# Computing M behind the denominators of a linear-attention kernel, in halves and single PSUM banks

## The chip, the core and the metric

One core of a Trainium2 chip runs the whole kernel. The metric is the device time of one execution in microseconds (us). Times are medians of three to six runs; the runs of the kernel before lay between 211.77 and 212.39 us beside the changed kernel. With one core there is no second die to compare, and every run used here was classed as fast.

Engines as the profile names them: PE is the matmul engine (TensorE), PEld its weight loads, DVE is VectorE, ACT is ScalarE, SP issues the DMAs. PSUM, where matmuls write, has eight banks.

## The reference, cut to what matters

```python
xn  = layernorm(x)                                  # 2048 tokens, D = 640
pq, pk = phi(q), phi(k)                             # phi(t) = 1e-6 + (t+1 where t>0, else exp(t)); 32 heads of 20
kv  = einsum("bhsd,bhse->bhde", pk, v)
num = einsum("bhqd,bhde->bhqe", pq, kv)
den = einsum("bhqd,bhd->bhq", pq, sum_s(pk)) + 1e-6
return x + (num / den) @ wo + gelu(xn @ w1 + b1) @ w2 + b2
```

The kernel never forms `num`. It multiplies the small block-diagonal `kv` by `wo` once, giving a 640x640 matrix **M**, and scales the rows of `pq` by 1/den. Each tile of 128 output tokens is then one accumulation in a pair of PSUM banks: 12 pairs of matmuls with W2 (the dense part), then 5 pairs of PQ·M.

## The kernel before: the parts that matter

```python
def q_chunk(c):                       # 512 tokens of q: 5 units, each 5 matmuls of 128x512
    for j in range(DT):
        b = take(1)                   # next bank of the ring of eight
        ...                           # matmuls into bank b
        phi(bank(b), b, 1, PQ[:, j, cc], r_PQ[c][j], [])   # ACT exp, then two DVE operations; frees b

def m_step():
    for j in range(DT):
        b = take(2)                   # a pair of banks
        for h in range(2):
            for i in range(2):
                for q in range(4):    # four matmuls on 32 columns of the array each
                    c0 = j + 32 * DT * q
                    fns.append(... e.matmul(bank(b + h, 0, HW)[32*q:32*q+32, :],
                        KVT[:, q + i, c0:c0 + 31*DT + 1:DT], Wo[:, q + i, h*HW:(h+1)*HW], ...))
        Pl.ins("tensor", fns, reads=[r_KVT, r_Wo], writes=B_[b:b + 2])
        Pl.ins("scalar", ... e.activation(halves(Msb[:, j, :]), pair(b), ACT.Copy),   # the eviction
               reads=B_[b:b + 2], writes=[r_M[j], r_zsum, r_zhl])
...                                   # cut
q_chunk(0); z_step(); kvt_step(); q_chunk(1); q_chunk(2)
m_step()
q_chunk(3)
...                                   # cut: inputs loaded again for the residual
bs = [out_w2(0)]                      # tile 0, W2 part
db = den_step()                       # 20 matmuls on 32 columns; DVE adds 1e-6, then the reciprocal
bs += [out_w2(1), out_w2(2, 0, JT // 2)]
rden_step(0, db)                      # broadcasts 1/den by a matmul; ACT copies, DVE scales PQ
out_w2(2, JT // 2, JT, bs[2])
for t in range(3):
    out_fin(t, bs[t])                 # PQ·M, residual, store
...                                   # cut: tiles 3 to 15, one after the other
```

A planner puts in the semaphore waits from the lists `reads` and `writes`. Each engine except PE also waits for its own earlier instruction where both write the same resource. Every eviction of M lists `r_zsum` and `r_zhl`, because M is stored over those buffers; so every eviction waits for the one before it (**self-wait**).

Of the kernel before, what the change touches and what calls it, by code (L numbers as in the profile page):

```python
# [6 lines left out]
ACT = mybir.ActivationFunctionType  # L7
# [105 lines left out]
def bass_parallel_sum__linear_attn_block__dense_activation_gelu__prompt_kernel(  # L113
# [4 lines left out]
    NT = S // P  # L118
# [3 lines left out]
    DT = D // P  # L122
    JT = F // P
    H = 32
    DH = D // H
    HW = D // 2
# [3 lines left out]
    Pl = Planner(nc)  # L130
# [6 lines left out]
    with contextlib.ExitStack() as es:  # L137
# [14 lines left out]
        KVT = W1f[:, DT * D:2 * DT * D].rearrange("p (k d) -> p k d", k=DT)  # L152
        Wqkv = sb("Wqkv", [P, DT, 3 * D], BF16)
        W2 = sb("W2", [P, JT, D], BF16)
        Wo = sb("Wo", [P, DT, D], BF16)
        Mf = sb("Msb", [P, DT * D], BF16)
        Msb = Mf[:].rearrange("p (k d) -> p k d", k=DT)
# [24 lines left out]
        B_ = [R_("bank%d" % i) for i in range(8)]  # L182
        ring = [0]

        def take(n):
            b = ring[0]
            if n == 2 and b % 2:
                b += 1
            b %= 8
            ring[0] = (b + n) % 8  # L190
            return b

        def bank(b, lo=0, hi=512):
            return ps[:, b * 512 + lo: b * 512 + hi]

        def pair(b):
            return ps[:, b * 512:(b + 2) * 512].rearrange("p (a n) -> p a n", a=2)[:, :, 0:HW]

        def halves(ap):
            return ap.rearrange("p (a n) -> p a n", a=2)  # L200
# [8 lines left out]
        r_Wq, r_Wk, r_Wv, r_W2, r_Wo = R_("Wq"), R_("Wk"), R_("Wv"), R_("W2"), R_("Wo")  # L209
# [11 lines left out]
        r_KVT = R_("KVT")  # L221
        r_M = [R_("M%d" % j) for j in range(DT)]
        r_zsum, r_zhl, r_z, r_ZB = R_("zsum"), R_("zhl"), R_("z"), R_("ZB")
# [30 lines left out]
        for c in range(2, NC):  # L254
# [18 lines left out]
               reads=[r_ident], writes=[r_ident])  # L273
# [108 lines left out]
        def h_first(jbs):  # L382
# [7 lines left out]
            for jb, b in zip(jbs, bs):  # L390
# [6 lines left out]
               reads=[r_warm], writes=[r_b1c])  # L397
# [47 lines left out]
        for t in range(TD, NT):  # L445
            if t > TD:
                ln_next(t)
            Pl.ins("sync", lambda e, t=t: e.dma_start_transpose(xnT[:, :, t * P:(t + 1) * P], xn_tm[:, t, :]),
                   reads=[r_xn[t]], writes=[r_xnT[t]], dma=True)
# [22 lines left out]
        for t in range(NT):  # L472
            b = take(2)
            fns = []
# [10 lines left out]
        for f in range(DT):  # L485
            b = take(2)
            for t in range(NT):
# [3 lines left out]
                    reads=[r_xn[t], r_PK[t]], writes=B_[b:b + 2])  # L491
            Pl.ins("scalar", lambda e, b=b, f=f: e.activation(halves(GTb[:, f, :]), pair(b), ACT.Copy),
                   reads=B_[b:b + 2], writes=[r_GT[f]] + r_W1)

        Pl.ins(v, lambda e: e.tensor_tensor(out=zsum, in0=PK[:, 0, :], in1=PK[:, 1, :], op=ALU.add),
               reads=[r_PK[0], r_PK[1]], writes=[r_zsum])
        for t in range(2, NT):
            Pl.ins(v, lambda e, t=t: e.tensor_tensor(out=zsum, in0=zsum, in1=PK[:, t, :], op=ALU.add),  # L498
                   reads=[r_PK[t], r_zsum], writes=[r_zsum])
# [3 lines left out]
               reads=[r_zsum, r_zhl], writes=[r_zhl])  # L503


        def q_chunk(c):
            cc = slice(c * CW, (c + 1) * CW)
            for j in range(DT):
                b = take(1)
                Pl.ins("tensor", [(lambda e, k=k, j=j, b=b: e.matmul(  # L510
                    bank(b), Wqkv[:, k, j:D:DT], xnT[:, k, cc],
                    start=(k == 0), stop=(k == DT - 1))) for k in range(DT)],
                    reads=[r_Wq] + r_xnT[c * CH:(c + 1) * CH], writes=[B_[b]])
                phi(bank(b), b, 1, PQ[:, j, cc], r_PQ[c][j], [])
# [20 lines left out]
                    out=KVT[:, t, e0[t]:e1[t]], in0=bank(b, 0, Wd[t]), in1=maskKV[t][:], op=ALU.mult),  # L535
                    reads=[B_[b], r_masks], writes=[r_KVT])

        def m_step():
            for j in range(DT):
                b = take(2)  # L540
                fns = []
                for h in range(2):
                    for i in range(2):
                        for q in range(4):
                            c0 = j + 32 * DT * q
                            fns.append(lambda e, t=q + i, q=q, i=i, h=h, b=b, c0=c0: e.matmul(  # L546
                                bank(b + h, 0, HW)[32 * q:32 * q + 32, :],
                                KVT[:, t, c0:c0 + 31 * DT + 1:DT], Wo[:, t, h * HW:(h + 1) * HW],
                                start=(i == 0), stop=(i == 1)))
                Pl.ins("tensor", fns, reads=[r_KVT, r_Wo], writes=B_[b:b + 2])  # L550
                Pl.ins("scalar", lambda e, b=b, j=j: e.activation(halves(Msb[:, j, :]), pair(b), ACT.Copy),
                       reads=B_[b:b + 2], writes=[r_M[j], r_zsum, r_zhl])

        def den_step():
            b = take(1)
            Pl.ins("tensor", [(lambda e, j=j, c=c: e.matmul(  # L556
                bank(b)[H * c:H * (c + 1), :], ZB[:, j, :], PQ[:, j, c * CW:(c + 1) * CW],
                start=(j == 0), stop=(j == DT - 1))) for j in range(DT) for c in range(NC)],
                reads=[r_ZB] + [r for q in r_PQ for r in q], writes=[B_[b]])
            Pl.ins(v, lambda e: e.tensor_single_scalar(den_sb[:], bank(b), 1e-6, ALU.add),  # L560
                   reads=[B_[b]], writes=[r_den])
            Pl.ins(v, lambda e: e.reciprocal(rden[:], den_sb[:]), reads=[r_den], writes=[r_rden])

            return b

        def rden_step(c, b):
            cc = slice(c * CW, (c + 1) * CW)
            s = c % 3
            rs = ek[:, s, 0:CW]
            Pl.ins("tensor", lambda e: e.matmul(bank(b), E4[:, c, :], rden[:], start=True, stop=True),  # L570
                   reads=[r_E4, r_rden], writes=[B_[b]])
            Pl.ins("scalar", lambda e: e.activation(rs, bank(b), ACT.Copy), reads=[B_[b]], writes=[r_ek[s]])  # L572
            for j in range(DT):
                Pl.ins(v, lambda e, j=j: e.tensor_tensor(out=PQ[:, j, cc], in0=PQ[:, j, cc], in1=rs, op=ALU.mult),  # L574
                       reads=[r_ek[s], r_PQ[c][j]], writes=[r_PQ[c][j]])
# [6 lines left out]
        def xb(t):  # L582
            Pl.ins(v, lambda e: e.tensor_tensor(out=x_res[:, t, :], in0=x_res[:, t, :], in1=b2bc[:], op=ALU.add),
                   reads=[r_xr[t // CH], r_b2], writes=[r_xb[t]])
# [3 lines left out]
        kvt_step()  # L588
        q_chunk(1)
        q_chunk(2)  # L590
        m_step()
        q_chunk(3)
        for c in range(NC):
            x_again(c)
# [2 lines left out]
        def mm(b, t, i, h):  # L597
            tok = slice(t * P, (t + 1) * P)
            l, r = ((HG[:, i, tok], W2[:, i, :]) if i < JT else (PQ[:, i - JT, tok], Msb[:, i - JT, :]))
            return lambda e: e.matmul(bank(b + h, 0, HW), l, r[:, h * HW:(h + 1) * HW],  # L600
                                      start=(i == 0), stop=(i == JT + DT - 1))

        def mm_reads(t, i):
            return [r_HG[t][i], r_W2] if i < JT else [r_PQ[t // CH][i - JT], r_M[i - JT]]

        def out_w2(t, lo=0, hi=JT, b=None):
            b = take(2) if b is None else b
            for i in range(lo, hi):
                Pl.ins("tensor", [mm(b, t, i, 0), mm(b, t, i, 1)], reads=mm_reads(t, i), writes=B_[b:b + 2],
                       mark=(i == JT - 1))  # L610
            return b

        def out_fin(t, b):
            s = t % 2
            for i in range(JT, JT + DT):
                Pl.ins("tensor", [mm(b, t, i, 0), mm(b, t, i, 1)], reads=mm_reads(t, i), writes=B_[b:b + 2],
                       mark=(i == JT + DT - 1))
            xb(t)
            Pl.ins(v, lambda e: e.tensor_tensor(out=halves(out_sb[:, s, :]), in0=pair(b),  # L619
                                                in1=halves(x_res[:, t, :]), op=ALU.add),  # L620
                   reads=B_[b:b + 2] + [r_xb[t]], writes=[r_out[s]])
            Pl.ins("sync", lambda e: e.dma_start(ov[t * P:(t + 1) * P, :], out_sb[:, s, :]),
                   reads=[r_out[s]], dma=True)
# [11 lines left out]
                Pl.ins("sync", lambda e, h=h, hs=hs: e.dma_start(ov[t * P:(t + 1) * P, hs], out_sb[:, h, 0:HW]),  # L635
                       reads=[r_out[h]], dma=True)

        bs = [out_w2(0)]
        db = den_step()
        bs += [out_w2(1), out_w2(2, 0, JT // 2)]  # L640
        rden_step(0, db)
        out_w2(2, JT // 2, JT, bs[2])
        for t in range(3):
            out_fin(t, bs[t])
        for t in range(3, NT - 1):
            b = out_w2(t)
            if t in (3, 6, 10):
                rden_step({3: 1, 6: 2, 10: 3}[t], take(1))
            out_fin(t, b)
# [41 lines left out]
```

## Time and profile before

| Reading | Value | Where |
|---|---|---|
| Time | 212.05 us (212.06 with the runs beside the change) | runs |
| PE busy | 205.5 us, 98% of the span | page, part 1 |
| M step, from its first matmul to the next PE line | 126.16 - 122.46 = 3.70 us | timeline |
| M step, matmuls alone (estimate) | 20 groups of four x 0.136 = 2.72 us | starts of the groups, here and in e12 |
| Evictions of M | 5 x 703 ns, about 0.79 us apart | groups by shape, timeline |

The page of the kernel before: engines' busy times, and the chain of work that ended last, by engine.

```profile
PE 205.5 (98%) x1585; PEld 140.1 (67%) x1585; DVE 110.5 (52%) x226; ACT 76.8 (36%) x145; POOL 20.5 (10%) x61
...
PE 86%; DVE 7%; DMA 4%; SPq 1%; issue 1%; DVEq 0%
```

The timeline around the M step, PE and two operations of DVE: start, duration, engine, source line, operation, out<-in, count, and in brackets the idle time just before it and what ended it.

```profile
121.72 0.81 PE L510 MATMUL ps<-xnT,Wqkv 128*128 128x512 bf16 x3
122.46 1.29 PE L546 MATMUL ps<-Wo,W 128*32 128x320 bf16 x32
123.10 0.69 DVE L467 SCALAR_TENSOR_TENSOR PQ<-ps,ek 128x512 bf16<-128x512 f32 x1
123.94 0.75 PE L546 MATMUL ps<-Wo,W 128*32 128x320 bf16 x16 [0.19 <-DVE PQ L467]
124.09 0.69 DVE L467 SCALAR_TENSOR_TENSOR PQ<-ps,ek 128x512 bf16<-128x512 f32 x1
124.93 1.29 PE L546 MATMUL ps<-Wo,W 128*32 128x320 bf16 x32 [0.24 <-DVE PQ L467]
126.16 1.06 PE L510 MATMUL ps<-xnT,Wqkv 128*128 128x512 bf16 x4
```

Both gaps end 0.14 to 0.15 us after a DVE operation on chunk 2 ends (123.79 and 124.79), so PE wanted a bank that DVE had not yet read. The bracketed idle understates the loss: a matmul's modelled end lies 0.30 us after its start, while the next ones start long before that. Four of these matmuls, one for each 32 columns of the array, start within 0.04 us of each other, and the next four 0.136 us later.

The activations by shape (count, busy us, mean ns, idle before).

```profile
L360 ACT ACTIVATE HG<-ps,b1c 128x512 bf16<-128x512 f32 x24 | 16.5, 687 | 9.6 <-PE ps L356 9.6
L360 ACT ACTIVATE HG<-ps,b1c 128x256 bf16<-128x256 f32 x30 | 14.2, 473 | 2.9 <-PE ps L356 0.9
L464 ACT ACTIVATE ek<-ps 128x512 bf16<-128x512 f32 x20 | 11.9, 597 | 11.2 <-PE ps L510 11.2
L551 ACT ACTIVATE Msb<-ps 128x640 bf16<-128x640 f32 x5 | 3.5, 703 | 0.5 <-PE ps L546 0.2
```

### The profile page before, as it was taken

The numbers are of one execution on the slowest core, as the hardware profiler recorded it, in microseconds if no ns is written. First come the engines' busy times: TensorE is split into PE (matmuls) and PEld (weight loads), VectorE is DVE, ScalarE is ACT, GpSimd is POOL, SyncE is SP. The second block draws the span as 40 slices with busy tenths as digits, with TensorE's granted clock in tenths as the row PEclk, the third lists the DMA queues.
The fourth block names the chain that finished last, engine by engine and source line by source line (L and its number), as shares of the span: only waits on it lengthen the run. The fifth ranks groups of instructions, "written<-read, shape, count | busy, mean of one in ns | idle before, by whom it ended". The sixth has DMA issues, their size and how long they took to land.

```text
span 210.7 us, 3883 instructions
## 1 busy us (share of the span) xinstructions
PE 205.5 (98%) x1585; PEld 140.1 (67%) x1585; DVE 110.5 (52%) x226; ACT 76.8 (36%) x145; POOL 20.5 (10%) x61
## 2 busy tenths in 40 slices
PE   7999999999999999999999999999999999999994
PEld 2689987444457777777666555677777777777772
DVE  4689981000008888999078866468451522263221
ACT  2579887666676554111253575110100100100000
POOL 2244557700000000000000000000000000000000
PEclk9999999999999999999999999999999999999999
DMA  5994758999000000000000000355411010001011
GB/s 165 340 349 99 101 111 101 347 321 346 10 0 0 0 3 0 0 3 0 0 0 3 0 5 0 124 138 170 163 35 54 9 65 31 31 31 34 31 62 33
DMA packets 21787, 17.46 MB, mean 83 GB/s; under 512 B 8713, under 2 KB 21769, under 8 KB 21769
## 3 DMA queue, kind: packets, MB, share of 16 engines
q1 hardware_dynamic: 21088, 16.72, 27.6%
q10 hardware_dynamic: 680, 0.49, 0.9%
q8 instruction: 12, 0.20, 0.4%
q14 instruction: 7, 0.05, 0.1%
HBM read 12.62 MB, written 2.62 MB: 72 GB/s over the span
## 4 chain that ended last, share of the span: by engine, by line
PE 86%; DVE 7%; DMA 4%; SPq 1%; issue 1%; DVEq 0%
PE ps L600 35%; PE ps L356 23%; PE ps L477 10%; PE ps L488 10%; PE ps L510 5%; DMA xPK<-in_A_x_dram 4%; DVE PQ L467 3%; DVE ek L465 1%; DVE W L534 1%; SPq L232 1%; PE ps L530 1%; PE ps L546 1%; DVE ZB L524 1%; PE ps L556 1%; DVE stats L313 0%
## 5 line engine op out<-in xcount | busy, mean ns | idle before, releaser
L600 PE MATMUL ps<-W,HG 128*128 128x320 bf16 x384 | 54.9, 299 | 0.0
L356 PE MATMUL ps<-xnT,W 128*128 128x128 bf16 (+2 forms) x435 | 52.0, 282 | 0.4 <-DMA W<-in_B_w_dram 0.4
L600 PEld LDWEIGHTS ps<-W,HG 128*128 128x128 bf16 x384 | 37.5, 98 | 15.2 <-issue 0.4
L356 PEld LDWEIGHTS ps<-xnT,W 128*128 128x128 bf16 x435 | 35.5, 98 | 16.1 <-DMA W<-in_B_w_dram 0.5
L360 ACT ACTIVATE HG<-ps,b1c 128x128 bf16<-128x128 f32 (+2 forms) x87 | 40.0, 492 | 13.2 <-PE ps L356 11.1
L465 DVE TENSOR_SCALAR ek<-ek 128x512 bf16<-128x512 bf16 (+1 forms) x36 | 10.9, 304 | 40.2 <-ACT ek L464 39.1
L464 ACT ACTIVATE ek<-ps 128x512 bf16<-128x512 f32 (+1 forms) x36 | 23.2, 644 | 20.4 <-PE ps L510 11.2
L619 DVE TENSOR_TENSOR out_sb<-ps,xnT 128x640 bf16<-128x640 f32 x15 | 12.4, 825 | 29.3 <-PE ps L600 26.2
L600 PE MATMUL ps<-Msb,PQ 128*128 128x320 bf16 x160 | 24.2, 299 | 0.0
L510 PE MATMUL ps<-xnT,Wqkv 128*128 128x512 bf16 x100 | 22.1, 379 | 0.0
L477 PE MATMUL ps<-Wqkv,xnT 128*128 128x320 bf16 x160 | 21.9, 299 | 0.0
L488 PE MATMUL ps<-xPK,xn_tm 128*128 128x320 bf16 x160 | 21.9, 299 | 0.0
L572 ACT ACTIVATE ek<-ps 128x512 bf16<-128x512 f32 x4 | 2.4, 597 | 49.2 <-PE ps L570 49.2
L600 PEld LDWEIGHTS ps<-Msb,PQ 128*128 128x128 bf16 x160 | 15.6, 98 | 6.3
L477 PEld LDWEIGHTS ps<-Wqkv,xnT 128*128 128x128 bf16 x160 | 15.7, 98 | 6.2
L488 PEld LDWEIGHTS ps<-xPK,xn_tm 128*128 128x128 bf16 x160 | 15.7, 98 | 6.1
L510 PEld LDWEIGHTS ps<-xnT,Wqkv 128*128 128x128 bf16 x100 | 11.6, 118 | 9.5 <-issue 0.2
L313 DVE BATCH_NORM_STATS2 stats<-xPK 128x6 f32<-128x320 bf16 x32 | 15.2, 475 | 3.5 <-DMA xPK<-in_A_x_dram 2.9
L467 DVE SCALAR_TENSOR_TENSOR PQ<-ps,ek 128x512 bf16<-128x512 f32 x20 | 13.8, 692 | 2.1
L467 DVE SCALAR_TENSOR_TENSOR xPK<-ps,ek 128x640 bf16<-128x640 f32 x16 | 13.2, 825 | 1.7
L498 DVE TENSOR_TENSOR Msb<-Msb,xPK 128x640 f32<-128x640 f32 x14 | 11.6, 825 | 0.5
L574 DVE TENSOR_TENSOR PQ<-PQ,ek 128x512 bf16<-128x512 bf16 x20 | 7.1, 419 | 9.0 <-ACT ek L572 9.0
(64 smaller groups left out, 89.3 us busy)
## 6 DMA issues: line engine op xcount, KB each, us to landing
xnT<-in_A_x_dram SPq DMA_DIRECT2D x4, 640.0 KB, 4.1
Wqkv<-in_A_wqkv_dram SPq DMA_DIRECT2D x3, 800.0 KB, 6.9
out_dram<-out_sb SPq DMA_DIRECT2D x15, 160.0 KB, 1.8
W<-in_B_w_dram SPq DMA_DIRECT2D x1, 1920.0 KB, 15.3
W<-in_B_w_dram SPq DMA_DIRECT2D x3, 480.0 KB, 7.6
xPK<-in_A_x_dram SPq DMA_DIRECT2D x2, 640.0 KB, 9.3
Wo<-in_A_wo_dram SPq DMA_DIRECT2D x1, 800.0 KB, 10.5
xPK<-in_A_x_dram SPq DMA_DIRECT2D x4, 160.0 KB, 4.5
```

Of the source, the lines that this page charges most:

```text
L313: Pl.ins(v, lambda e: e.bn_stats(stats[:, s, 6 * h:6 * h + 6], x_in[:, t, h * HW:(h + 1) * HW]), reads=[r_x[t]], writes=[r_stats[s]])
L356: Pl.ins("tensor", [(lambda e, k=k: e.matmul(bank(b, 0, w), W1[:, k, jb * P:(jb + 1) * P], xnT[:, k, tok], start=(k == 0), stop=(k == DT - ...
L360: Pl.ins("scalar", lambda e: e.activation(HG[:, jb, tok], bank(b, 0, w), ACT.Gelu_apprx_tanh, bias=b1c[:, jb:jb + 1]), reads=[B_[b], r_b1c ...
L464: Pl.ins("scalar", lambda e: e.activation(e2, src, ACT.Exp), reads=br, writes=[r_ek[s]])
L465: Pl.ins(v, lambda e: e.tensor_scalar(et, et, 1.0, 1e-6, ALU.min, ALU.add), reads=[r_ek[s]], writes=[r_ek[s]])
L467: Pl.ins(v, lambda e: e.scalar_tensor_tensor(out=d2, in0=src, scalar=0.0, in1=e2, op0=ALU.max, op1=ALU.add), reads=br + [r_ek[s]], writes= ...
L477: fns.append(lambda e, k=k, h=h, b=b, t=t: e.matmul(bank(b + h, 0, HW), xnT[:, k, t * P:(t + 1) * P], Wqkv[:, k, D + h * HW:D + (h + 1) * ...
L488: Pl.ins("tensor", [(lambda e, t=t, h=h, b=b, f=f: e.matmul(bank(b + h, 0, HW), xn_tm[:, t, f * P:(f + 1) * P], PK[:, t, h * HW:(h + 1) * ...
L498: Pl.ins(v, lambda e, t=t: e.tensor_tensor(out=zsum, in0=zsum, in1=PK[:, t, :], op=ALU.add), reads=[r_PK[t], r_zsum], writes=[r_zsum])
L510: Pl.ins("tensor", [(lambda e, k=k, j=j, b=b: e.matmul(bank(b), Wqkv[:, k, j:D:DT], xnT[:, k, cc], start=(k == 0), stop=(k == DT - 1))) fo ...
L600: return lambda e: e.matmul(bank(b + h, 0, HW), l, r[:, h * HW:(h + 1) * HW], start=(i == 0), stop=(i == JT + DT - 1))
L619: Pl.ins(v, lambda e: e.tensor_tensor(out=halves(out_sb[:, s, :]), in0=pair(b), in1=halves(x_res[:, t, :]), op=ALU.add), reads=B_[b:b + 2] ...
```

## The change

The intent: take M out of the place where PE meets DVE's backlog, let chunk 3 follow chunk 2 at once, and compute M after the denominators, where the reciprocal takes DVE 3.35 us anyway. At that place tile 0 holds a pair of banks and the denominators hold one, so M gets single banks, four in turn. The output order changes with it: the W2 part of tile 2 no longer comes ahead of the first PQ·M.

```diff
-        def m_step():
-            for j in range(DT):
-                b = take(2)
-                ...                                     # cut: both halves of row block j
+        def m_half(j, h, b):
+            ...                                         # cut: the same eight matmuls, one half
+            Pl.ins("tensor", fns, reads=[r_KVT, r_Wo], writes=[B_[b]])
+            Pl.ins("scalar", lambda e: e.activation(Msb[:, j, h * HW:(h + 1) * HW], bank(b, 0, HW), ACT.Copy),
+                   reads=[B_[b]], writes=[r_M[j], r_zsum, r_zhl])
...
         q_chunk(2)
-        m_step()
         q_chunk(3)
...
-        bs = [out_w2(0)]
+        b0 = out_w2(0)
         db = den_step()
-        bs += [out_w2(1), out_w2(2, 0, JT // 2)]
+        mb = [(b0 + 2 + i) % 8 for i in range(6) if (b0 + 2 + i) % 8 != db][:4]
+        for i in range(2 * DT):
+            m_half(i // 2, i % 2, mb[i % 4])
+        ring[0] = (b0 + 6) % 8
+        b1 = out_w2(1, 0, JT // 2)
         rden_step(0, db)
-        out_w2(2, JT // 2, JT, bs[2])
-        for t in range(3):
-            out_fin(t, bs[t])
-        for t in range(3, NT - 1):
+        out_w2(1, JT // 2, JT, b1)
+        out_fin(0, b0)
+        out_fin(1, b1)
+        for t in range(2, NT - 1):
```

Here `b0` is bank 6, `db` bank 0, M's banks are 1, 2, 3, 4, and tile 1 takes 4 and 5. Bank 4 thus serves both M (halves 3 and 7, counted from 0) and tile 1.

More of the change, by code (lines that the diff above doesn't have):

```diff
@@ L536, in kvt_step @@
                     reads=[B_[b], r_masks], writes=[r_KVT])
-        def m_step():
-            for j in range(DT):
-                b = take(2)
-                fns = []
-                for h in range(2):
-                    for i in range(2):
-                        for q in range(4):
-                            c0 = j + 32 * DT * q
-                            fns.append(lambda e, t=q + i, q=q, i=i, h=h, b=b, c0=c0: e.matmul(
-                                bank(b + h, 0, HW)[32 * q:32 * q + 32, :],
-                                KVT[:, t, c0:c0 + 31 * DT + 1:DT], Wo[:, t, h * HW:(h + 1) * HW],
-                                start=(i == 0), stop=(i == 1)))
-                Pl.ins("tensor", fns, reads=[r_KVT, r_Wo], writes=B_[b:b + 2])
-                Pl.ins("scalar", lambda e, b=b, j=j: e.activation(halves(Msb[:, j, :]), pair(b), ACT.Copy),
-                       reads=B_[b:b + 2], writes=[r_M[j], r_zsum, r_zhl])
+        def m_half(j, h, b):
+            fns = []
+            for i in range(2):
+                for q in range(4):
+                    c0 = j + 32 * DT * q
+                    fns.append(lambda e, t=q + i, q=q, i=i, c0=c0: e.matmul(
+                        bank(b, 0, HW)[32 * q:32 * q + 32, :],
+                        KVT[:, t, c0:c0 + 31 * DT + 1:DT], Wo[:, t, h * HW:(h + 1) * HW],
+                        start=(i == 0), stop=(i == 1)))
+            Pl.ins("tensor", fns, reads=[r_KVT, r_Wo], writes=[B_[b]])
+            Pl.ins("scalar", lambda e: e.activation(Msb[:, j, h * HW:(h + 1) * HW], bank(b, 0, HW), ACT.Copy),
+                   reads=[B_[b]], writes=[r_M[j], r_zsum, r_zhl])
         def den_step():
```

## The prediction

> **What bounds the kernel.** TensorE: PE busy 98% of the 210.7 us span, granted clock 0.9 or more in every slice (page, parts 1 and 2). From 126 us on, the chain of waits is PE alone. In the output stage neither DVE nor ACT holds PE up. The one leak that the change touches is the M step: its timeline runs from 122.46 to the next PE line at 126.16, 3.70 us, for 80 matmuls. Its unbroken runs (32 in 1.29 us, the last lasting 0.30) give 0.033 us each, so 2.67 us of work and about 1.0 us of waiting: the idle before L546 is put down to DVE (PQ, 0.4 us in two waits) and ACT (Msb L551, 0.5 us).
>
> **What the change does.** q chunk 3 follows chunk 2 directly; tile 0's W2 part and the denominators start about 3.7 us earlier; the same 80 M matmuls come after the denominators in ten halves through four single banks. Five 128x640 evictions (703 ns each) become ten 128x320. Activations of 128x256 and 128x512 take 473 and 687 ns (groups by shape), 0.83 ns per column; from the 512-wide copy at 597 ns I estimate 0.44 us for 320. Evictions also wait for the one before, since every one writes the same z resources: three L551 take 2.29 us, so the pitch is 0.79, 0.09 above the duration. I expect a pitch of 0.53 us and 5.3 us on ACT, against 4.0 before.
>
> The Trainium skill, "Perfetto Trace Analysis", section "Optimizing Scalar/DVE Operations", says that ScalarE has an overhead per instruction, whose write acknowledgement normally overlaps the next instruction; this trace agrees about the overhead (0.17 us left at zero columns by the line above), and the self-wait takes the overlap away.
>
> **Critical path.** Let M start at T. A half is 0.27 us of PE; the first eviction starts at T+0.53 and ends at T+0.97; eviction i ends at T+0.97+0.53i. PE needs about 0.15 us after a release (DVE ends 123.79, PE starts 123.94). Halves 4 to 9 then go at ACT's pace, the last starting near T+3.8. Tile 1's W2 part takes a pair whose first bank is the fourth M bank, so it waits for eviction 7: T+4.68, PE at T+4.83. M thus holds PE for 4.8 us against 3.7 before, +1.1 us; about 0.1 may come back at the edges. The waits after chunk 2 vanish, but dearer ones replace them. The reciprocal (3.35 us) is done at about T+4.2, before PE asks for it at T+6.5; PQ's scaling has the same six pairs of W2 matmuls to hide behind; tile 2 reuses tile 0's banks with some 0.3 us to spare.
>
> **Prediction:** 213.1 us, 80% range 212.4 to 213.8. Faster by over 2%: 0.01; within 2%: 0.98; slower by over 2%: 0.01.
>
> **What would show it.** Evictions of M: ten at about 0.44 us, 0.53 apart. PE idle before the M matmuls and before tile 1's first W2 matmul put down to ACT Msb, about 2.1 us together; no DVE wait before M. The denominators' matmuls near 131.1 us; tile 1's W2 near 137.2. Rden matmul without idle before it; tile pitch in the output stage unchanged at 4.6 us.
>
> **What would make it wrong.** Evictions faster or free of the self-wait: at a pitch of 0.44, the loss is only 0.4 us. A PE wait of chunk 3 for DVE's backlog (3 us behind PE at 115 us). The reciprocal or PQ's scaling becoming exposed: up to 1 us more.

## The result

The changed kernel takes 212.87 us (212.74 to 213.57, six runs) against 212.06 us (211.77 to 212.39, six runs). The ratio is 1.0043, 95% interval 1.0027 to 1.0060: it is 0.4% slower, well inside 2%. Ratios here are the mean time of one kernel's fast runs over that of the other's of the same rounds, so not quite the ratio of the medians quoted.

The page of the changed kernel, same lines:

```profile
PE 204.6 (97%) x1575; PEld 139.9 (66%) x1585; DVE 110.0 (52%) x226; ACT 77.8 (37%) x150; POOL 20.5 (10%) x61
...
PE 93%; DMA 3%; ACT 1%; issue 1%; ACTq 0%; DVE 0%
```

In the chain DVE has fallen from 7% to 0%, and ACT is new in it with 1%. The shares alone would suggest a gain. (The ten missing PE records of 1585 are lost records; the weight loads are complete.) The timeline of the new M step, PE, PEld and ACT:

```profile
130.64 1.26 PE L553 MATMUL ps<-PQ,ZB 128*32 128x512 bf16 x20
131.51 1.43 PEld L543 LDWEIGHTS ps<-Wo,W 128*32 128x32 bf16 x40
131.73 4.11 PE L543 MATMUL ps<-Wo,W 128*32 128x320 bf16 x80
132.23 3.62 ACT L548 ACTIVATE Msb<-ps 128x320 bf16<-128x320 f32 x7 [4.14 <-PE ps L543]
133.25 0.17 PEld L543 LDWEIGHTS ps<-Wo,W 128*32 128x32 bf16 x8 [0.30 <-ACT Msb L548]
133.77 0.17 PEld L543 LDWEIGHTS ps<-Wo,W 128*32 128x32 bf16 x8 [0.36 <-ACT Msb L548]
134.30 0.17 PEld L543 LDWEIGHTS ps<-Wo,W 128*32 128x32 bf16 x8 [0.36 <-ACT Msb L548]
...
136.21 1.50 ACT L548 ACTIVATE Msb<-ps 128x320 bf16<-128x320 f32 x3 [0.37 <-PE ps L543]
136.70 1.47 PEld L596 LDWEIGHTS ps<-W,HG 128*128 128x128 bf16 x12 [1.17 <-ACT Msb L548]
136.70 3.65 PE L596 MATMUL ps<-W,HG 128*128 128x320 bf16 x24 [0.86 <-ACT Msb L548]
```

The seven evictions of the first ACT row are (3.62 - 0.438) / 6 = 0.53 us apart. From the sixth half on, the weight loads come in eights at the same 0.53 us: PE works for 0.27 us and waits for ACT. Tile 1's W2 matmuls start at 136.70, just after the eighth eviction, which holds the shared bank. M holds PE 136.70 - 131.73 = **4.97 us**, against 3.70 before: 1.27 us more.

**How to compare runs to a tenth.** The start of the kernel, where the first inputs and weights arrive by DMA, differs by up to 0.7 us between profiled runs: the transposes of token tile 2 started between 11.8 and 12.5 us. So I also give the *aligned stretch*: from those transposes (five on PE, near 12 us) to the start of the last five PQ·M matmuls. Before it is 206.96 - 12.32 = 194.64 us; after, 207.53 - 11.84 = 195.69 us. The difference is 1.05 us, so 0.22 us of the 1.27 came back outside M. The stages show where: the 50 matmuls of chunks 1 and 2 took 0.09 us more to reach the M step before than 50 times the 0.2158 us between their starts, and the denominators 1.19 us before (134.94 to 136.13) against 1.09 us now (130.64 to 131.73); together that is 0.19 of the 0.22.

### The profile page after: what moved, and what is told of

Its sections match the earlier page's. It is cut to its first block, busy times and chain, and to the rows that moved or that the text cites. A ratio compares the mean times of both kernels' runs of the same rounds, so it can differ in the third digit from the quotient of the medians.

```text
span 211.2 us, 3883 instructions
## 1 busy us (share of the span) xinstructions
PE 204.6 (97%) x1575; PEld 139.9 (66%) x1585; DVE 110.0 (52%) x226; ACT 77.8 (37%) x150; POOL 20.5 (10%) x61
## 4 chain that ended last, share of the span: by engine, by line
PE 93%; DMA 3%; ACT 1%; issue 1%; ACTq 0%; DVE 0%
PE ps L596 35%; PE ps L356 24%; PE ps L477 10%; PE ps L488 10%; PE ps L510 10%; DMA W<-in_B_w_dram 3%; ACT Msb L548 1%; PE ps L530 1%; PE ps L543 1%; PE ps L553 1%; PE ps L386 0%; PE ps L340 0%; ACTq L236 0%; DVE out_sb L628 0%; PE ps L518 0%
## 5 line engine op out<-in xcount | busy, mean ns | idle before, releaser
L360 ACT ACTIVATE HG<-ps,b1c 128x128 bf16<-128x128 f32 (+2 forms) x87 | 40.1, 493 | 12.5 <-PE ps L356 10.4
L510 PE MATMUL ps<-xnT,Wqkv 128*128 128x512 bf16 x97 | 21.4, 379 | 0.2
```

The costliest lines, as they stand in the source:

```text
L360: Pl.ins("scalar", lambda e: e.activation(HG[:, jb, tok], bank(b, 0, w), ACT.Gelu_apprx_tanh, bias=b1c[:, jb:jb + 1]), reads=[B_[b], r_b1c ...
L510: Pl.ins("tensor", [(lambda e, k=k, j=j, b=b: e.matmul(bank(b), Wqkv[:, k, j:D:DT], xnT[:, k, cc], start=(k == 0), stop=(k == DT - 1))) fo ...
```

## The experiments

Theory A: in the changed kernel PE waits for ACT's pace, 0.53 us for each eviction, through the release of banks. Rival B: the place behind the denominators costs by itself (reciprocal, PQ's scaling or the repeated loads exposed). Rival C: ten small evictions cost more than five large ones, whatever they wait for. Each run had five rounds beside the kernel before, and all results were correct. They were made in four batches on three chips, where the kernel before had medians of 212.12 (e1 to e4), 212.01 (e5 to e8), 212.24 (e9 to e11) and 212.17 us (e12): across batches compare the ratios or the aligned stretch, not the medians. The aligned stretch comes from one profiled run each.

| Run | M holds PE, us | Aligned stretch, us | Median, us | Ratio to before (95%) |
|---|---|---|---|---|
| before | 3.70 | 194.64 | 212.06 | 1 |
| changed | 4.97 | 195.69 | 212.87 | 1.0043 (1.0027 to 1.0060) |
| e1: no self-wait | 3.30 | 194.02 | 211.37 | 0.9959 (0.9947 to 0.9971) |
| e2: pairs, late | 3.92 | 194.63 | 212.23 | 1.0004 (0.9989 to 1.0018) |
| e3: halves, early | 3.43 | 194.37 | 211.83 | 0.9982 (0.9967 to 0.9997) |
| e4: five banks | 4.04 | 194.75 | 212.38 | 1.0002 (0.9989 to 1.0015) |
| e5: interleaved | mixed | 195.95 | 213.63 | 1.0073 (1.0058 to 1.0088) |
| e6: interleaved, no self-wait | mixed | 195.95 | 213.43 | 1.0069 (1.0054 to 1.0083) |
| e7: halves, early, no self-wait | 3.43 | 194.38 | 211.94 | 0.9997 (0.9982 to 1.0011) |
| e8: shifted | 4.69 | 195.41 | 213.11 | 1.0048 (1.0034 to 1.0062) |
| e9: five banks, no self-wait | 3.04 | 193.76 | 211.38 | 0.9961 (0.9919 to 1.0003) |
| e10: denominators split | 4.97 | 196.56 | 213.90 | 1.0068 (1.0032 to 1.0104) |
| e11: before, no self-wait | 3.70 | 194.66 | 212.32 | 0.9988 (0.9949 to 1.0027) |
| e12: six banks, no self-wait | 2.82 | 193.53 | 211.40 | 0.9975 (0.9936 to 1.0014) |

### e1: no self-wait

```diff
-  writes=[r_M[j], r_zsum, r_zhl]
+  writes=[r_M[2 * j + h]] + ([r_zsum, r_zhl] if j + h == 0 else [])
```

Only the first eviction must wait for the readers of the old buffers; ACT starts its evictions in program order, in this trace as in the others, so the rest are covered. PQ·M reads both halves' resources.

> The changed kernel, but each M eviction has its own resource, so ten evictions no longer wait for the one before on ScalarE. Theory A (PE waits for ScalarE's pace in the M step, and the pace is 0.53 us because of the self-wait): pitch falls to 0.35-0.44 us, the M step from 4.97 us to 3.5-4.1, total 211.5-212.0 us. Rival B (the place behind the denominators is what costs: reciprocal, scaling or reloads exposed): pitch falls, but the time only moves into another wait and stays 212.7-213.0. Rival C (it is the small evictions' fixed cost): pitch stays near 0.44-0.53, total 212.3-212.9.

```profile
131.80 3.11 PE L543 MATMUL ps<-Wo,W 128*32 128x320 bf16 x80
132.30 3.40 ACT L548 ACTIVATE Msb<-ps 128x320 bf16<-128x320 f32 x10 [4.14 <-PE ps L543]
135.10 1.80 PE L596 MATMUL ps<-W,HG 128*128 128x320 bf16 x12 [0.19 <-ACT Msb L548]
```

The ends of the ten evictions are now (3.40 - 0.44) / 9 = 0.33 us apart (the first lasts 0.44 us), less than the 0.43 to 0.54 us that one lasts: they overlap. M fell by 1.67 us to 3.30, and the aligned stretch by the same 1.67. Pitch, M and time (211.37 us) all came out a little under the ranges I gave A, and the time is under the kernel before. B falls: nothing took the gain back. C falls too: there are still ten evictions.

### e2: the old form at the new place

```diff
-  for i in range(2 * DT):
-      m_half(i // 2, i % 2, mb[i % 4])
+  m_step([(b0 + 4) % 8, (b0 + 6) % 8])    # five pairs, two pairs of banks in turn, 128x640 evictions
```

> The new place with the old form: five pairs of banks and five 128x640 evictions behind the denominators, two pairs in turn, tile 1 then taking the second pair. Theory A: evictions 0.79 us apart; tile 1's W2 waits for the fourth of five (T+4.0), so the M step holds PE 4.0-4.1 us, total 211.9-212.1 us. Rival B (the place itself costs): 212.7-213.0, as changed.

M took 3.92 us and the aligned stretch 194.63, equal to the kernel before. The evictions were (3.88 - 0.703) / 4 = 0.79 us apart; five with a self-wait are cheaper than ten. So the new place with the old form costs nothing net. M was a little shorter than expected for A, and the median, 212.23, a little longer; the start of the kernel may have done this, but it is not shown.

### e3: the new form at the old place

```diff
-  m_step()
+  for i in range(2 * DT):
+      m_half(i // 2, i % 2, take(1))      # between chunks 2 and 3, all eight banks in turn
```

> The old place with the new form: ten halves between query chunks 2 and 3, single banks out of all eight in turn. Theory A: eight banks let PE run ahead of ScalarE's pace, so M holds PE 2.8-3.0 us instead of 3.7; the evictions' 5.3 us hide behind chunk 3; total 211.1-211.5 us, under the kernel before. Rival C (ten small evictions cost by themselves): 212.3-213, as changed. Rival B does not touch this run: 212.1 or less.

A miss in size: M fell only to 3.43 us, not to 2.8 to 3.0, and the time only to 211.83 us.

```profile
122.10 2.11 PE L543 MATMUL ps<-Wo,W 128*32 128x320 bf16 x56
123.74 0.69 DVE L467 SCALAR_TENSOR_TENSOR PQ<-ps,ek 128x512 bf16<-128x512 f32 x1
124.58 1.02 PE L543 MATMUL ps<-Wo,W 128*32 128x320 bf16 x24 [0.37 <-DVE PQ L467]
```

Seven halves run without a break; the eighth needs the bank of chunk 2's last unit, and starts 0.15 us after DVE has read it (124.43). I had counted ACT's pace and the number of banks, but not which bank DVE would free last.

Four aligned stretches now form a square: before 194.64 us, the new place alone (e2) 194.63, the new form alone (e3) 194.37, both together (changed) 195.69. Neither place nor form loses time by itself; time is lost only where both meet, ten self-waiting evictions through four banks (e1 above takes away the self-wait, e4 below adds a bank).

### e4: five banks

```diff
-  mb = [...][:4];  m_half(i // 2, i % 2, mb[i % 4])
+  mb = [(b0 + d) % 8 for d in (3, 4, 5, 6)] + [db]
+  m_half(i // 2, i % 2, mb[(0, 1, 2, 3, 4, 0, 1, 2, 4, 0)[i]])   # the bank shared with tile 1: once
```

> The changed kernel with five banks for M, the denominators' bank being the fifth once VectorE has read it, and the bank that tile 1 needs used once only, for the fourth half. Evictions keep their 0.53 us pitch. Theory A, with the shared bank as the last link: M holds PE 3.8-4.0 us instead of 4.97, total 211.8-212.0. If only the pace counts and not which bank tile 1 waits for: last half still bound at about 4.3 us, 212.2-212.4. Rival B: 212.7-213.0.

```profile
131.71 2.52 PE L543 MATMUL ps<-Wo,W 128*32 128x320 bf16 x64
134.81 1.00 PE L543 MATMUL ps<-Wo,W 128*32 128x320 bf16 x16 [0.58 <-ACT Msb L548]
135.75 1.80 PE L596 MATMUL ps<-W,HG 128*128 128x320 bf16 x12
```

M took 4.04 us, 0.93 less than in the changed kernel, and the aligned stretch fell by 0.94, though the evictions kept their 0.53 us. The trace no longer puts the wait of tile 1's first W2 matmul down to ACT. The median of 212.38 lies in the range of the second possibility, that the pace alone counts; M itself lies close to the first, and the aligned stretch agrees with it. What counts is which eviction PE must wait for, and the pace up to that one.

### e5 and e6: halves between the W2 matmuls of tile 1

```diff
-  for i in range(2 * DT): m_half(i // 2, i % 2, mb[i % 4])
-  b1 = out_w2(1, 0, JT // 2);  rden_step(0, db);  out_w2(1, JT // 2, JT, b1)
+  mb = [(b0 + d) % 8 for d in (3, 4, 5)];  b1 = take(2)
+  for i in range(JT):
+      out_w2(1, i, i + 1, b1)                     # one pair of W2 matmuls
+      if i < 2 * DT: m_half(i // 2, i % 2, mb[i % 3])
+      if i == 7: rden_step(0, db)
```

> The changed kernel, but each of the ten M halves is put between two pairs of tile 1's W2 matmuls, in three banks that tile 1 does not use; the self-wait of the evictions stays (0.53 us apart). One half and one W2 pair are 0.54 us of PE, so PE should hardly wait. If M's cost behind the denominators is only PE waiting for ScalarE's pace with nothing else to do: tile 1's W2 with all of M takes 6.0-6.3 us (work 5.9, plus 0.2 for the denominators' broadcast), against 4.97 + 3.5 in the changed kernel; about 2.2 us less, total 210.5-211.0. If evictions and W2 matmuls disturb each other, or the scaling of PQ is exposed by evictions ahead of it on ScalarE: 211.5 or more.

> The same with the evictions' self-wait taken away (pitch could be 0.33 us). If PE's work alone is left in this stage, nothing more is to be had: within 0.3 us of the interleaved run with the self-wait. If ScalarE's pace still held PE there: 0.3-0.6 us less than it.

This was to hide ACT's pace entirely, and it was the largest miss: 213.63 and 213.43 us, slower than the kernel before; the aligned stretch is 0.26 us over the changed kernel's too. The timeline of e5:

```profile
132.98 0.11 PEld L596 LDWEIGHTS ps<-W,HG 128*128 128x128 bf16 x2 [0.24 <-issue]
132.99 0.45 PE L596 MATMUL ps<-W,HG 128*128 128x320 bf16 x2
133.11 0.44 ACT L548 ACTIVATE Msb<-ps 128x320 bf16<-128x320 f32 x1 [4.66 <-PE ps L543]
133.36 0.16 PEld L543 LDWEIGHTS ps<-Wo,W 128*32 128x32 bf16 x8 [0.26 <-issue]
133.36 0.48 PE L543 MATMUL ps<-Wo,W 128*32 128x320 bf16 x8
133.77 0.11 PEld L596 LDWEIGHTS ps<-W,HG 128*128 128x128 bf16 x2 [0.24 <-issue]
```

PE waits for no engine ("issue"), and ACT has time to spare. Yet a W2 pair and a half take 133.77 - 132.98 = 0.79 us together (0.785 on average over the first eight), where their matmuls need 0.272 + 0.272. At every change of kind, the weights of the next matmul are loaded only about when the last matmul before ends, instead of well ahead of it. Taking the self-wait away (e6) left the aligned stretch at 195.95 us to the hundredth, so ACT has no part in it.

The Trainium skill, "TensorEngine Tiling (Array Packing)", section "Key Properties", has a reason that fits: "Changing tiling mode (not just tile) drains the TensorE". W2 matmuls use the array whole (128*128 in the profile), M and the denominators use it in columns of 32 (128*32). The page gives no cost. Here it is (0.785 - 0.543) / 2 = 0.12 us for each change. A change of weights and banks without a change of mode shows no such gap: from the denominators to M, both in columns of 32, the weight loads of the changed kernel start at 131.51, 0.22 us ahead of M's first matmul.

### e7: halves early, no self-wait

The edit is that of e1, made in e3.

> Ten halves between chunks 2 and 3 (as in the earlier run, 211.83 us, M 3.43 us) without the self-wait. There the trace put PE's wait down to VectorE's backlog on chunk 2, whose bank the eighth half needs. If so: evictions faster, but M still holds PE 3.3-3.45 us and the total stays at 211.7-211.9. If ScalarE's pace was the limit there too: M 2.8-3.0 us, total 211.2-211.4.

M stayed at 3.43 us and the aligned stretch at 194.38 (e3: 194.37), while the ten evictions fell from 5.19 to 3.50 us in all. The trace puts the wait before the eighth half down to ACT here; but PE again starts 0.15 us after DVE's last operation on chunk 2 (124.70 to 124.85), and a faster ACT changed nothing. At the old place DVE's backlog is the limit, and ACT's pace is not.

### e8: ScalarE's instructions shifted

```diff
+  for k in range(16):      # tiny, into ACT's idle time before the first eviction
+      Pl.ins("scalar", lambda e, k=k: e.activation(scr[:, k:k+1], warm[:, 0:1], ACT.Copy), ...)
```

> The changed kernel with 16 tiny ScalarE instructions put before the first M eviction, into 4.1 us in which ScalarE is idle. In the changed kernel and in the run with five banks, the eighth eviction starts 0.37 us late with nothing in the trace that it waits for. If that pause belongs to a place in ScalarE's instruction stream: it now falls among the tiny ones, evictions come 0.53 us apart throughout, M holds PE 4.65 us, total 0.2-0.4 us under the changed kernel (212.5-212.7). If it belongs to the eighth eviction (data, bank, PE): it stays there, M 4.97 us, 212.8-213.0.

```profile
132.19 4.11 PE L544 MATMUL ps<-Wo,W 128*32 128x320 bf16 x80
132.69 5.20 ACT L549 ACTIVATE Msb<-ps 128x320 bf16<-128x320 f32 x10 [2.66 <-PE ps L544]
136.88 1.80 PE L597 MATMUL ps<-W,HG 128*128 128x320 bf16 x12 [0.58 <-ACT Msb L549]
```

The 0.37 us before the eighth eviction is gone: ten evictions in one row, 0.53 us apart, M at 4.69 us, the aligned stretch 0.28 us shorter. So the pause does not belong to the eighth eviction. A place in ACT's instruction stream fits: e4 and e10, with the same ACT instructions up to there, have the pause; e8, with 16 more, and e1, e9 and e12, without the self-waits, have none. But it was not seen among the tiny ones either (they start 0.093 us apart throughout), so what ACT does there, and where it went, is not shown. The median of 213.11 us missed my range: the aligned trace resolves 0.3 us, the medians do not.

### e9 and e12: five and six banks, no self-wait

The edits of e1 and e4 together; e12 also lends out the second bank of tile 1's pair, once:

```diff
-  mb = [...(3, 4, 5, 6)] + [db];                  order (0, 1, 2, 3, 4, 0, 1, 2, 4, 0)
+  mb = [...(3, 4, 5, 6)] + [db, (b0 + 7) % 8];    order (0, 1, 2, 3, 4, 5, 0, 1, 2, 4)
```

> Five banks and no self-wait together, M in one block behind the denominators. Evictions 0.33 us apart; only the last two halves wait a little. M holds PE 2.8-3.0 us against 4.97 in the changed kernel and 3.30 with the self-wait alone taken away; total 210.9-211.2, the fastest so far. If some other limit than ScalarE's release of banks stood behind the 3.30: M stays at 3.3, 211.3-211.5.

> As the run with five banks and no self-wait, but six banks: both banks of tile 1's pair are lent once each, to the fourth and sixth half, so that no half should have to wait for an eviction. M: 2.67 us of matmuls and one switch back to full width of about 0.11-0.12, 2.80 us against 3.04 with five banks; no idle before M's matmuls put down to ScalarE. Total 211.0-211.3; aligned at the transposes before tile 2's first W1 product, some 0.24 us less than with five banks. If a limit other than bank release is left: M stays at 3.0.

```profile
131.30 1.26 PE L553 MATMUL ps<-PQ,ZB 128*32 128x512 bf16 x20
132.39 2.89 PE L543 MATMUL ps<-Wo,W 128*32 128x320 bf16 x80
132.89 3.40 ACT L548 ACTIVATE Msb<-ps 128x320 bf16<-128x320 f32 x10 [4.14 <-PE ps L543]
135.21 3.65 PE L596 MATMUL ps<-W,HG 128*128 128x320 bf16 x24
```

In e12 the 80 matmuls run as one block: 135.21 - 132.39 = 2.82 us, close to the 2.80 expected; 20 groups of four x 0.136 = 2.72 us (estimate, starts of the groups) is the matmuls' own pace, and 0.10 is left for the one change of mode at the end. e9 had 3.04. The aligned stretch of e12, 193.53 us, is 2.16 us under the changed kernel and 1.11 under the kernel before. Their median times (211.38 and 211.40) hardly differ from that of e1, and both are a little over the ranges expected. Both had one run over 213 us (213.13 and 213.73, granted clock 0.992 where the other runs have 0.998 or more), which widens their intervals to just over 1. In the rounds of e9 to e11 the kernel before had two such runs (213.91 and 214.09); they pull each of these three ratios down by about 0.0016. Of the three, only e1 is shown faster than both kernels by timing; e12 is shown shorter by its trace alone.

### e10: the price of a change of mode, by itself

```diff
-  b0 = out_w2(0);  db = den_step()
+  # tile 0: pairs 0 to 7, then den(j=0), pair 8, den(1), pair 9, den(2), pair 10, den(3), pair 11, den(4)
```

> The changed kernel, with the 20 denominator matmuls cut into five groups of four that stand between the last W2 pairs of tile 0. Same work, nothing new to wait for, eight more switches between full-width matmuls and matmuls on 32 columns. The interleaved runs took 0.785 us for a half and a pair that need 0.54, which would be 0.12 us for each of 20 switches. If the switch is what costs: +1.0 us (0.9-1.1), total 213.7-214.0, weight loads of both kinds starting 0.24-0.26 us after the load before them. If it was something of M's halves (their banks, their evictions): no change, 212.8-213.0.

```profile
130.26 0.10 PEld L554 LDWEIGHTS ps<-PQ,ZB 128*32 128x32 bf16 x4 [0.26 <-issue]
130.26 0.40 PE L554 MATMUL ps<-PQ,ZB 128*32 128x512 bf16 x4
130.59 0.11 PEld L599 LDWEIGHTS ps<-W,HG 128*128 128x128 bf16 x2 [0.23 <-issue]
130.59 0.45 PE L599 MATMUL ps<-W,HG 128*128 128x320 bf16 x2
```

The same matmuls with eight more changes of mode, and no eviction or M near them: the aligned stretch grew by 0.87 us, 0.11 us for each, a little under the 0.9 to 1.1 expected. The gaps in the weight loads are those of e5. The change of mode is the cost, not M.

### e11: the kernel before, no self-wait

```diff
-  writes=[r_M[j], r_zsum, r_zhl]
+  writes=[r_M[j]] + ([r_zsum, r_zhl] if j == 0 else [])
```

> The kernel before with its five M evictions freed of the self-wait and nothing else. Its trace put the two waits inside M on VectorE's backlog from chunk 2. If so: pitch of the evictions falls, but M keeps holding PE 3.6-3.7 us, total 211.8-212.2, same as before. If ScalarE's pace was the limit there too: M 3.0-3.3 us, total 211.4-211.7.

```profile
124.11 0.75 PE L546 MATMUL ps<-Wo,W 128*32 128x320 bf16 x16 [0.19 <-DVE PQ L467]
125.11 1.29 PE L546 MATMUL ps<-Wo,W 128*32 128x320 bf16 x32 [0.25 <-DVE PQ L467]
126.33 1.24 PEld L510 LDWEIGHTS ps<-xnT,Wqkv 128*128 128x128 bf16 x7 [0.25 <-issue]
126.58 1.24 PE L510 MATMUL ps<-xnT,Wqkv 128*128 128x512 bf16 x5 [0.18 <-issue]
```

M took 126.33 - 122.63 = 3.70 us and the aligned stretch 194.66, as before (3.70 and 194.64). (The record of chunk 3's first matmul is lost here, so its weight load stands for it.) The evictions do run faster, yet PE's gaps still end 0.15 us after DVE. The self-wait cost the kernel before nothing, and the changed kernel 1.67 us.

## Why the prediction was right

**The time.** 213.1 us was predicted, with 212.4 to 213.8; 212.87 was measured. The predicted loss of about 1.0 us is 1.05 in the aligned stretch and 0.8 between medians.

**The mechanism.** "Evictions of M: ten at about 0.44 us, 0.53 apart" came out at 0.438 and 0.53, but for the pause. PE's waiting of "about 2.1 us together" was 4.97 - 2.72 = 2.25 us, the change of mode included (the matmuls' own 2.67 us were 2.72). The bank that tile 1 waits for was named, and e4 and e12 confirm it. The self-wait was named as what makes the pace, and e1 confirms it. "no DVE wait before M", the reciprocal hidden, the broadcast of 1/den without idle time, and an unchanged tile pitch (4.62 us in both traces) all came out. The denominators ("near 131.1") and tile 1 ("near 137.2") both came about 0.5 us earlier, because the whole profile started as much earlier.

**Sizes were off, and partly cancelled.** That the loss came within 0.05 us of the prediction is in part luck.

- M was put at 4.83 us and took 4.97, with two errors of opposite sign. PE was taken to need 0.15 us after a release, as it does after DVE's; after an eviction by ACT it started 0.05 us after its end (136.65 to 136.70). That, and a first eviction 0.03 us earlier, is why M without the pause takes 4.69 (e8). ACT's pause, which was not foreseen, adds 0.28.
- "about 0.1 may come back at the edges": it was 0.22. The order before had four changes of array mode around M and the denominators; the changed order, with both side by side, has two. At 0.11 us each this accounts for it, and the two stages quoted under the result show 0.19 of it. I had seen the small gaps and not asked what they were.
- "at a pitch of 0.44, the loss is only 0.4 us": without the self-wait the pitch is 0.33 because evictions overlap, and the loss becomes a gain (e1). The end of one eviction is not the earliest start of the next.

The Trainium skill, "TensorEngine Tiling (Array Packing)", section "PSUM Bottleneck", warns that tiling speeds up the matmuls but not the evacuation of PSUM. A half is 0.27 us of PE and was 0.53 us of ACT. The move took PE away from DVE's backlog, but put M where nothing else fills PE while ACT empties four banks.

Three things stay open: what ACT's pause is; whether e9 and e12 are faster than e1 in measured time; and what the slower runs at a clock of 0.992 are.

## What to carry to other kernels

When matmuls on part of the array fill PSUM faster than one engine empties it, list for each bank the eviction that its next user waits for; order the banks so that this one is early, and free the evictions of waits for each other that the data do not need. Keep matmuls of one array mode together: here each change cost 0.11 to 0.12 us, and interleaving meant to hide a wait cost more than the wait. A wait removed at one place is a gain only if the work meets no longer wait at the next.

## What the Trainium skill lacked or had wrong

- "TensorEngine Tiling (Array Packing)", section "Key Properties", names the drain at a change of mode, but no cost. Between 128*128 and 128*32 it is 0.11 us (e10) to 0.12 us (e5) a change.
- "Perfetto Trace Analysis", section "Optimizing Scalar/DVE Operations", says that the write acknowledgement overlaps the next instruction. The runs agree that instructions overlap (ends 0.33 us apart where one lasts 0.43 to 0.54 us, e1), but neither this page nor "ScalarE: Activation LUTs" says what it costs when an instruction waits for the one before it on its own engine: 0.53 us apart, 0.20 more.
- The same section puts ScalarE's overhead on PSUM near 51 ns, and the profiled latency at about twice that. With 0.83 ns a column (from the activations by shape), 0.06 us are left of the pitch of 0.33, which agrees; of the duration of 0.44, 0.17 are left, which is about three times 51 ns and not twice. So the prediction's word that the trace agrees holds for there being an overhead, not for its size. This concerns that section's figures alone.
- No page that I found gives the idle 0.37 us on ScalarE before the eighth eviction (changed kernel, e4 and e10; gone in e8), 0.28 us more than between the others.
